# Router tables of the first two expert slots made on GpSimd instead of VectorE, with another deal of the last heads' products

## The chip, the cores and the metric

The kernel runs on one core of one Trainium2 chip. The metric is the device time of one launch in microseconds (us), the median of several runs. The core's engines are TensorE (PE in the profile, its weight loads PEld), VectorE (DVE), ScalarE (ACT), GpSimd (POOL) and SyncE (SP), which here only issues transfers. Each engine works through its own instructions in the order written, and waits for others by semaphores.

## What is computed

Attention with a threshold below each row's maximum, then a mixture of eight experts with one expert for each token, then a dense feed-forward network. The reference, shortened:

```python
# q, k, v: (4, 8, 576, 64); 2304 tokens of width 512
scores = q @ k.T / 8
scores = where(scores >= scores.max(-1) - tau, scores, -1e9)
x = softmax(scores) @ v                         # rows: tokens, columns: 8 heads x 64
logits = x @ w_gate + modality_bias[modality_id]
e_idx, gate_w = argmax(logits), softmax(logits)[e_idx]
for e in range(8):
    mask = e_idx == e
    out[mask] = gate_w[mask] * (relu(x[mask] @ w1[e]) @ w2[e])
h = out @ w_in
result = (h * sigmoid(1.702 * h)) @ w_out
```

## The kernel before, in words

**Attention** (`Attention.run`) works on 16 pairs of heads, four pairs to a batch of 576 tokens. A pair has nine units of 128 query rows; an iteration `it` of the loop handles two units, so there are 72 full iterations (`it` 0 to 71) and one that only drains; the last batch begins at `it` 54. In each iteration TensorE makes the score products of two units (`qk`, L244, eight matmuls, or twelve where a pair's last unit falls in it), transposes the weights of the iteration before (`trans`, L330 and following), and takes some products with the values from the queue `avq` (`av_items`, L374 and L380) and at most one row item from the queue `rowq`. VectorE makes each unit's maximum (L272) and, after ScalarE's exponential (L278), its mask (L302). Two units' scores are in flight, each in PSUM banks of its own, so score products wait for the mask of two units earlier.

A **row item** (`row_items`, L414) transposes 128 finished tokens of four heads back into rows on TensorE, together with their eight router logits; ScalarE copies them out (`xr`, L419), GpSimd multiplies them by the softmax's reciprocals (L422 for the rows `xrow`, L427 for the logits `lgt`), and SyncE writes the rows to DRAM (L433, two transfers). `xr` and `xrow` have two buffers each.

How much of each queue an iteration takes is a table by hand. For the last batch these are `AVL` (value products) and `ROWL` (row items), with one entry for each of `it` 54 to 72. What is left in the queues runs after the loop in `att.tail`, between the steps that prepare the first expert slot.

**The router** (`Router`) gives each token a place in slots of 512 tokens. The first two slots (phase "A") are filled from batches 0 to 2 while the last batch's attention runs. Its steps wait in a list `side`, from which `sides` takes a few at fixed points of each iteration; `None` in that list ends a turn. After batch 2's logits the list holds, in order: `NROW` empty turns, the expert choice (`gate_items`, VectorE), running sums (`pre`, GpSimd, L707), and `assign("A")`: `ranks` (three small matmuls, L742 to L744, copied by ScalarE into `rs` and `cnt`), then `pages`, `starts`, `limits`, `slots`, `inside`, `counted`, `places`, `digits`, which turn ranks into places, then `high`, `low` and `values`, which make one-hot rows `R` and `OL`, then `sum_up` (15 small matmuls, L893, on TensorE), and `lists`, which gives the token indices `igaA`. With these GpSimd gathers the first slot's rows from DRAM (L1080). From `pages` to `values` nearly all is VectorE's, mixed in between its maxima and masks.

After attention the **first expert slot** needs its gathered rows scaled (L1241, VectorE), transposed (L965, TensorE) and split into two parts (ScalarE and VectorE); then its first products (L993) start, and from there the expert slots and the dense network keep TensorE at work to the end.

The lines that the change touches are the tables (L32, L33), `row_items`, `sides`, and the closures of `assign`.

Of the kernel before, what the change touches and what calls it, by code (L numbers as in the profile page):

```python
# [21 lines left out]
NE = 8  # L22
# [9 lines left out]
AVL = (2, 2, 3, 5, 0, 2, 3, 2, 1, 2, 2, 3, 5, 0, 2, 3, 3, 2, 5)  # L32
ROWL = (1, 1, 1, 0, 1, 1, 1, 1, 1, 0, 0, 0, 0, 1, 1, 1, 1, 1, 1)  # L33
# [6 lines left out]
NBW = 6  # L40
# [9 lines left out]
class Attention:  # L50
# [347 lines left out]
    def row_items(self, b, hh):  # L398
# [153 lines left out]
class Router:  # L552
# [19 lines left out]
    def setup_items(self, tmp_pool):  # L572
# [25 lines left out]
        self.pages = T([128, NE], "pages")  # L598
        self.place = T([128, NB * PG // 128], "place")
# [36 lines left out]
        def order():  # L636
# [4 lines left out]
            nc.gpsimd.tensor_scalar_mul(self.pages, e, float(PG))  # L641

# [78 lines left out]
    def assign(self, ph, gate):  # L721
# [5 lines left out]
        t = {}  # L727
        T = lambda shape, name, dt=F32: wk.tile(shape, dt, name=name)
# [8 lines left out]
        R = T([128, n, 2, nh], "R", BF16)  # L737

# [9 lines left out]
        def pages():  # L748

            if not first:  # L750
                nc.vector.tensor_sub(cnt, cnt, self.lim)
# [4 lines left out]
            nc.vector.tensor_tensor(  # L756
                cmp, cnt.unsqueeze(2).broadcast_to([128, NE, top]), pg.unsqueeze(1).broadcast_to([128, NE, top]),
                op=ALU.is_ge if first else ALU.is_gt)
            yield
            nc.vector.tensor_reduce(out=f, in_=cmp, axis=AX.X, op=ALU.add)  # L760
            yield

        def starts():
            x = T([128, NE, NE], "fx")
            nc.vector.tensor_mul(x, self.before, f.unsqueeze(1).broadcast_to([128, NE, NE]))
            yield
            nc.vector.tensor_reduce(out=excl, in_=x, axis=AX.X, op=ALU.add)
            yield
            nc.vector.tensor_scalar(base, excl, float(PG), 1.0, op0=ALU.mult, op1=ALU.add)
            yield  # L770

        def limits():
            if first:
                nc.vector.tensor_scalar(self.lim, excl, -1.0, float(NA), op0=ALU.mult, op1=ALU.add)
                yield
                nc.vector.scalar_tensor_tensor(out=self.lim, in0=self.lim, scalar=0.0, in1=f, op0=ALU.max, op1=ALU.min)
                yield
                nc.vector.tensor_add(end, excl, self.lim)
                yield
                nc.vector.tensor_scalar_mul(self.lim, self.lim, float(PG))  # L780
                yield
            else:
                nc.vector.tensor_add(end, excl, f)
                yield
                nc.vector.tensor_sub(base, base, self.lim)
                yield
                self.range = self.c.tile([128, 2], I32, name="range")
                nc.vector.tensor_scalar(self.range[:, 1:2], end[:, NE - 1:NE], float(NB_STATIC), None, op0=ALU.max)
                yield

        def slots():
            cmp = T([128, ns, NE], "cmp")
            nc.vector.tensor_tensor(
                cmp, end.unsqueeze(1).broadcast_to([128, ns, NE]),
                self.iota[:, 0:ns].unsqueeze(2).broadcast_to([128, ns, NE]), op=ALU.is_le,
            )
# [3 lines left out]
            nc.vector.tensor_reduce(out=ef, in_=cmp, axis=AX.X, op=ALU.add)  # L800
            yield
            ei = self.c.tile([128, ns], I32, name="ei" + ph)
            nc.vector.tensor_scalar(ei, ef, float(NE - 1), None, op0=ALU.min)
# [38 lines left out]
        def inside():  # L842
            nc.vector.tensor_tensor(ok, rs, be(self.lim), op=ALU.is_lt if first else ALU.is_ge)
            yield
            nc.vector.tensor_mul(ok, ok, self.oh[:, 0:n])
            yield

        def counted():
            nc.vector.tensor_add(rs, rs, be(base))
            yield  # L850
            nc.vector.tensor_mul(ok, ok, rs)
            yield

        def places():
            pos = T([128, n], "pos")
            nc.vector.tensor_reduce(out=pos, in_=ok, axis=AX.X, op=ALU.add)
            yield
            pint = T([128, n], "pint", I32)
            nc.vector.tensor_scalar_add(pint, pos, -1.0)
# [3 lines left out]
        def digits():  # L863
            pint = t["pint"]
# [8 lines left out]
        def low(c0, c1):  # L873
            nc.vector.tensor_tensor(
# [4 lines left out]
        def high():  # L879
            nc.vector.tensor_tensor(  # L880
                R[:, :, 1, :], self.iota[:, 0:nh].unsqueeze(1).broadcast_to([128, n, nh]),
                plf[:, 0].unsqueeze(2).broadcast_to([128, n, nh]), op=ALU.is_equal,
            )
# [30 lines left out]
        def compact():  # L914
# [17 lines left out]

        rest = [] if first else [None]
# [649 lines left out]
```

## Time and profile before

| | |
|---|---|
| median of 3 runs | 935.27 us (934.87 to 935.39) |
| profiled execution | 936.12 us, its span 934.4 us, mean granted clock 0.995 |
| PE busy | 904.0 us, 97% of the span |
| DVE, ACT, POOL busy | 512.2 (55%), 446.8 (48%), 223.1 us (24%) |
| chain that ended last | PE 81%, issue 7%, DVE 4%, DMA 3%, ACT 2%, POOL 2% |
| PE idle from 260 to 300 us | 4.6 us of 40 |
| PE idle from 310 to 320 us | 4.5 us of 10 |

Times within the span count from its first instruction; 1.7 us of the profiled execution lie outside it. Busy shares are averages over stages that differ: the attention loop ends at about 309 us, the expert slots follow from about 319 us. A wait is put down to the instruction that released it. Durations on POOL are rough.

### The profile page before, as it was taken

The page shows a single profiled execution, that of the slowest core. Times are in us where ns is not written, and L with a number is a line of the kernel's source. Part 1 is how long each engine was busy: PE and PEld are TensorE (multiplying, and loading weights), DVE is VectorE, ACT ScalarE, POOL GpSimd, SP SyncE. Part 2 cuts the span into 40 slices and gives each one's busy share as a digit, 9 for nine tenths or more (in the row PEclk, how much of TensorE's full clock was granted, in tenths as well). Part 3 has the DMA queues.
Part 4 walks back from the last instruction along what each step waited for, and adds up shares of the span by engine and source line. Part 5 has one row for each costly group of instructions (what it writes and reads, how often), then busy time and mean ns, then how long its engine had stood idle before and what let it go on. Part 6 is the DMA issues. An engine that isn't in the chain of part 4 may idle for free.

```text
span 934.4 us, 13874 instructions
## 1 busy us (share of the span) xinstructions
PE 904.0 (97%) x5031; PEld 740.6 (79%) x5031; DVE 512.2 (55%) x1129; ACT 446.8 (48%) x788; POOL 223.1 (24%) x299
## 2 busy tenths in 40 slices
PE   8999999999998799999999999999999999999994
PEld 7777777777776588778888988888888888888894
DVE  6788788888789485477777568821111111211110
ACT  6677777777666443446455545532223222222221
POOL 4837556566602501010530000010001000100100
PEclk9999999999999999999999999999999999999998
DMA  7755774664411644466666244410001000100100
GB/s 211 174 145 148 204 199 115 156 164 119 109 43 26 206 141 143 153 204 203 196 207 233 94 140 147 150 46 1 25 22 46 6 12 6 46 1 1 46 1 25
DMA packets 64522, 100.70 MB, mean 108 GB/s; under 512 B 10596, under 2 KB 35970, under 8 KB 64450
## 3 DMA queue, kind: packets, MB, share of 16 engines
q1 hardware_dynamic: 61138, 89.84, 33.5%
q0 software_dynamic: 3312, 9.94, 3.2%
q8 instruction: 41, 0.67, 0.3%
q14 instruction: 31, 0.25, 0.1%
HBM read 63.97 MB, written 17.11 MB: 87 GB/s over the span
## 4 chain that ended last, share of the span: by engine, by line
PE 81%; issue 7%; DVE 4%; DMA 3%; ACT 2%; POOL 2%; SPq 1%; POOLq 0%; ACTq 0%
PE tr L993 28%; PE sc L1018 19%; PE sc L1037 9%; PE sc L244 8%; PE av L374 6%; PE tr L330 5%; PE av L380 2%; PE tr L414 2%; DVE e L272 1%; ACT e L278 1%; DMA cv_raw<-in_moe_w_in_dram 1%; SPq L179 1%; PE tr L352 1%; DVE E L302 1%; DMA xg<-y_first 1%
## 5 line engine op out<-in xcount | busy, mean ns | idle before, releaser
L1230 DVE TENSOR_TENSOR hl<-sg,hh 128x512 fp32r<-128x512 f32 (+1 forms) x80 | 51.1, 638 | 260.3 <-ACT hh L1228 257.9
L1227 ACT ACTIVATE sg<-tr 128x512 f32<-128x512 f32 (+1 forms) x80 | 44.3, 554 | 225.4 <-PE tr L993 225.4
L278 ACT ACTIVATE e<-e,thr 128x576 f32<-128x576 f32 x144 | 109.7, 776 | 77.4 <-DVE e L272 74.8
L272 DVE TENSOR_SCALAR_CACHE_REDUCE e<-sc,taue 128x576 f32<-128x576 f32 x144 | 113.4, 815 | 38.4 <-PE sc L244 37.7
L1018 PE MATMUL sc<-wo_h,hh 128*128 128x512 f32 x288 | 112.2, 390 | 0.0
L1018 PE MATMUL sc<-wo_l,hh 128*128 128x512 f32 x288 | 112.2, 390 | 0.0
L1018 PE MATMUL sc<-wo_h,hl 128*128 128x512 f32 x288 | 112.0, 389 | 0.0
L244 PE MATMUL sc<-kA,qT 128*128 128x288 f32 x320 | 99.3, 331 | 5.8 <-DVE E L302 3.8
L302 DVE SCALAR_TENSOR_TENSOR E<-sc,thr,e 128x576 f32<-128x576 f32 x128 | 100.7, 813 | 4.7 <-ACT e L278 3.8
L244 PE MATMUL sc<-kB,qT 128*128 128x288 f32 x320 | 87.9, 295 | 1.7 <-DMA kB<-kB 1.2
L993 PE MATMUL tr<-xl,wi_h 128*128 128x512 f32 (+1 forms) x320 | 78.7, 368 | 0.0
L993 PE MATMUL tr<-xh,wi_l 128*128 128x512 f32 (+1 forms) x320 | 78.7, 368 | 0.0
L993 PE MATMUL tr<-xh,wi_h 128*128 128x512 f32 (+1 forms) x320 | 78.6, 368 | 0.0
L374 PE MATMUL av<-AT,V 128*64 128x288 f32 x512 | 76.9, 419 | 0.5 <-ACT xT L381 0.5
L244 PEld LDWEIGHTS sc<-kA,qT 128*128 128x128 f32 x320 | 60.1, 188 | 21.0 <-DVE E L302 14.1
L332 ACT COPY AT<-tr 128x512 f32<-128x512 f32 x128 | 68.3, 577 | 0.1
L330 PE MATMUL tr<-ident,E 128*128 128x128 f32 x512 | 67.6, 272 | 0.0
L993 PEld LDWEIGHTS tr<-xh,wi_h 128*128 128x128 f32 x320 | 57.6, 188 | 11.1
L993 PEld LDWEIGHTS tr<-xh,wi_l 128*128 128x128 f32 x320 | 56.9, 189 | 10.0
L993 PEld LDWEIGHTS tr<-xl,wi_h 128*128 128x128 f32 x320 | 56.9, 189 | 10.0
L1018 PEld LDWEIGHTS sc<-wo_h,hl 128*128 128x128 f32 x288 | 54.0, 188 | 11.4
L244 PEld LDWEIGHTS sc<-kB,qT 128*128 128x128 f32 x320 | 60.2, 188 | 3.0 <-issue 1.3
(220 smaller groups left out, 1567.2 us busy)
## 6 DMA issues: line engine op xcount, KB each, us to landing
ra<-in_moe_w_dram SPq DMA_DIRECT2D x20, 512.0 KB
rb<-in_moe_w_dram SPq DMA_DIRECT2D x20, 512.0 KB, 5.2
F<-in_kq_dram SPq DMA_DIRECT2D x15, 640.0 KB, 4.6
cv_raw<-in_moe_w_in_dram SPq DMA_DIRECT2D x16, 512.0 KB, 4.8
cv_raw<-in_moe_w_out_dram SPq DMA_DIRECT2D x16, 512.0 KB, 4.3
V<-in_vp_dram SPq DMA_DIRECT2D x16, 320.0 KB, 5.0
kA<-kA SPq DMA_DIRECT2D x15, 320.0 KB, 3.3
kB<-kB SPq DMA_DIRECT2D x15, 320.0 KB, 3.6
```

What stands on the lines that cost most here:

```text
L244: m = nc.tensor.matmul(self.banks[:, bank, 0:288], l, d[kk][:, c0 + k0:c0 + k0 + 288], start=(i == 0), stop=(i == len(ops) - 1),).ins
L272: self.read(u, nc.vector.tensor_scalar(e, d["sc", w], self.taue[:, 0:1], 3.0e38, op0=ALU.add, op1=ALU.min, accum_out=thr))
L278: self.nc.scalar.activation(d["e", w], d["e", w], ACTF.Exp, bias=d["thr", w][:, 0:1], scale=-1.0)
L302: self.read(u, nc.vector.scalar_tensor_tensor(out=E.rearrange("p (a c) -> p a c", a=2), in0=d["sc", w], scalar=d["thr", w][:, 0:1], in1=d[ ...
L330: nc.tensor.transpose(tp[:, kc * 128:(kc + 1) * 128], E[:, k0 + kc * 128:k0 + (kc + 1) * 128], self.ident)
L332: return lambda: nc.scalar.copy(AT[:, h, :, c * 128:(c + 1) * 128], tp.rearrange("p (k c) -> p k c", k=4))
L374: nc.tensor.matmul(d["av"][h * 64:(h + 1) * 64, 0:288], d["V"][:, h, kc, :], d["AT"][:, h, kc, cols], start=(kc == 0), stop=False, skip_gr ...
L993: nc.tensor.matmul(hps[:, 0:T], w[:, kd, :], blk[x][:, kd, 0:T], start=(i == 0), stop=(i == 11))
L1018: nc.tensor.matmul(y, h[:, cs], w, start=(f == 0 and i == 0), stop=(f == blk["nf"] - 1 and i == 2))
L1037: nc.tensor.matmul(blk["y"][d], w[:, ds], h[:, 0:T], start=(f == 0 and i == 0), stop=(f == last and i == 2))
L1227: nc.scalar.activation(sg, hps, ACTF.Gelu_apprx_sigmoid)
L1230: return [upper, lambda: nc.vector.tensor_sub(hl, sg, hh.bitcast(F32))]
```

## The change

The steps from `pages` to `values` of phase "A" move from VectorE to GpSimd. GpSimd compares by a subtraction and a comparison with zero (`compare`), and sums along a row by halving (`fold`); `limits` takes seven instructions in place of four; `digits` counts the multiples of 128 below a place in place of an integer shift; and each of the 15 columns of `OL` is an instruction of its own with a scalar for each partition. `double` lets a point of `sides` take two of these steps. `NROW` empty turns become one for batch 2. A row item's logits are now made ahead of its rows. `False` in the list ends every point but an iteration's last, so that `sum_up` comes at an iteration's end. `AVL` and `ROWL` have new entries.

```diff
-AVL = (2, 2, 3, 5, 0, 2, 3, 2, 1, 2, 2, 3, 5, 0, 2, 3, 3, 2, 5)
-ROWL = (1, 1, 1, 0, 1, 1, 1, 1, 1, 0, 0, 0, 0, 1, 1, 1, 1, 1, 1)
+AVL = (2, 2, 3, 2, 3, 2, 3, 2, 1, 2, 2, 3, 3, 2, 2, 3, 3, 2, 5)
+ROWL = (0, 1, 0, 1, 1, 1, 1, 1, 1, 0, 0, 0, 0, 1, 0, 1, 0, 1, 0)
...
             nc.gpsimd.tensor_mul(
+                lgt[0:w, kc, hs, :].rearrange("p (a c) e -> p a c e", a=2),
+                xr[0:w, :, 128:144].rearrange("p a (c e) -> p a c e", c=2),
+                rr.unsqueeze(3).broadcast_to([w, 2, 2, NE]),
+            )
+            nc.gpsimd.tensor_mul(
                 xrow[0:w].rearrange("p (a c d) -> p a c d", a=2, c=2),
                 xr[0:w, :, 0:128].rearrange("p a (c d) -> p a c d", c=2),
                 rr.unsqueeze(3).broadcast_to([w, 2, 2, 64]),
-            )
-            nc.gpsimd.tensor_mul(
-                lgt[0:w, kc, hs, :].rearrange("p (a c) e -> p a c e", a=2),
-                xr[0:w, :, 128:144].rearrange("p a (c e) -> p a c e", c=2),
-                rr.unsqueeze(3).broadcast_to([w, 2, 2, NE]),
             )
             for u in range(2 if kc < 4 else 1):
                 nc.sync.dma_start(xd[b, 2 * kc + u][:, hh * 256:(hh + 1) * 256], xrow[u * 64:(u + 1) * 64, :])
...
-                self.side.extend([None] * NROW + items + self.router.after_batch(b, gate))
+                self.side.extend([None] * (1 if b == B - 2 else NROW) + items + self.router.after_batch(b, gate))
...
+            if f is False:
+                if not turn:
+                    break
+                side.pop(0)
+                continue
...
+            nc.gpsimd.tensor_scalar_mul(self.hundreds, e, 128.0)
...
+        def compare(out, x, y, op):
+
+            if not first:
+                return nc.vector.tensor_tensor(out, x, y, op=op)
+            nc.gpsimd.tensor_sub(out, x, y)
+            nc.gpsimd.tensor_scalar(out, out, 0.0, None, op0=op)
+
+        def fold(out, x):
+
+            if not first:
+                return nc.vector.tensor_reduce(out=out, in_=x, axis=AX.X, op=ALU.add)
+            m = x.shape[-1]
+            while m > 2:
+                k = m // 2
+                nc.gpsimd.tensor_add(x[:, :, 0:k], x[:, :, 0:k], x[:, :, m - k:m])
+                m -= k
+            nc.gpsimd.tensor_add(out, x[:, :, 0], x[:, :, 1])
...
-                nc.vector.tensor_scalar(self.lim, excl, -1.0, float(NA), op0=ALU.mult, op1=ALU.add)
+                E.tensor_scalar(self.lim, excl, -1.0, float(NA), op0=ALU.mult, op1=ALU.add)
                 yield
-                nc.vector.scalar_tensor_tensor(out=self.lim, in0=self.lim, scalar=0.0, in1=f, op0=ALU.max, op1=ALU.min)
+                more = T([128, NE], "more")
+                E.tensor_scalar(self.lim, self.lim, 0.0, None, op0=ALU.max)
                 yield
-                nc.vector.tensor_add(end, excl, self.lim)
+                E.tensor_sub(more, self.lim, f)
                 yield
-                nc.vector.tensor_scalar_mul(self.lim, self.lim, float(PG))
+                E.tensor_scalar(more, more, 0.0, None, op0=ALU.max)
+                yield
+                E.tensor_sub(self.lim, self.lim, more)
+                yield
+                E.tensor_add(end, excl, self.lim)
+                yield
+                E.tensor_scalar_mul(self.lim, self.lim, float(PG))
                 yield
...
+            if first:
+                pos, g = t["pos"], T([128, n, nh], "ge")
+                hundreds = self.hundreds.unsqueeze(1).broadcast_to([128, n, nh])
+                E.tensor_sub(g, pos.unsqueeze(2).broadcast_to([128, n, nh]), hundreds)
+                E.tensor_scalar(g, g, 0.0, None, op0=ALU.is_ge)
+                yield
+                fold(plf[:, 0], g)
+                E.tensor_scalar_add(plf[:, 0], plf[:, 0], -1.0)
+                yield
+                E.tensor_scalar_mul(plf[:, 1], plf[:, 0], 128.0)
+                E.tensor_sub(plf[:, 1], pos, plf[:, 1])
+                yield
+                return
...
         def low(c0, c1):
+            if first:
+                for c in range(c0, c1):
+                    nc.gpsimd.tensor_scalar(OL[:, c], self.iota, plf[:, 1, c:c + 1], None, op0=ALU.is_equal)
+                return
             nc.vector.tensor_tensor(
                 OL[:, c0:c1], self.iota.unsqueeze(1).broadcast_to([128, c1 - c0, 128]),
                 plf[:, 1, c0:c1].unsqueeze(2).broadcast_to([128, c1 - c0, 128]), op=ALU.is_equal,
             )
 
         def high():
-            nc.vector.tensor_tensor(
+            compare(
                 R[:, :, 1, :], self.iota[:, 0:nh].unsqueeze(1).broadcast_to([128, n, nh]),
-                plf[:, 0].unsqueeze(2).broadcast_to([128, n, nh]), op=ALU.is_equal,
-            )
+                plf[:, 0].unsqueeze(2).broadcast_to([128, n, nh]), ALU.is_equal)
 
         def values(i):
-            eng = nc.gpsimd if first and not i else nc.vector
-            eng.tensor_mul(R[:, :, i, :], R[:, :, 1, :], self.idp[:, i, 0:n].unsqueeze(2).broadcast_to([128, n, nh]))
+            E.tensor_mul(R[:, :, i, :], R[:, :, 1, :], self.idp[:, i, 0:n].unsqueeze(2).broadcast_to([128, n, nh]))
...
+        def double(g):
+
+            def go():
+                it, end = g(), object()
+                while next(it, end) is not end and next(it, end) is not end:
+                    yield
+
+            return go if first else g
...
-            None, ranks, pages, starts, limits, slots, inside, counted, places, digits, *rest, high,
+            None, ranks, *map(double, (pages, starts, limits, slots, inside, counted, places, digits)), *rest, high,
             lambda: (low(0, 5), values(0)), *rest, lambda: (low(5, 10), values(1)), *rest, lambda: low(10, n), gate,
-            *[None] * (1 if first else NBW), lambda: sum_up(0, n), lists,
+            *([None, False] if first else [None] * NBW), lambda: sum_up(0, n), lists,
```

Where the instructions stand now. On **TensorE in iteration 66**, the three matmuls of `ranks` follow the transposes, one iteration earlier than before (in iteration 67 they stood between the same kinds of rows); `oh` are the choices, `pre` their running sums, `tri` and `ones` constants, `tr` a PSUM bank. Now:

```order
L244 MATMUL sc<-kB,qT_137 128x288
L330 MATMUL tr<-ident,E 128x128 x8
L768 LDWEIGHTS tri
L768 MATMUL tr<-oh,tri 128x120
L769 LDWEIGHTS ones
L769 MATMUL tr<-pre,ones 128x120
L770 LDWEIGHTS ones
L770 MATMUL tr<-pre,ones 128x8
L374 MATMUL av<-AT,V 64x288 x6
```

Iteration 66 also has six of the value products' instructions in place of eight and their closing one (L380), which stand in iteration 67 now.

On **TensorE**, the 15 pairs of `sum_up` stood in **iteration 71**, behind that iteration's transposes (first pair shown):

```order
L244 MATMUL sc<-kA,qT_135 128x288
L244 MATMUL sc<-kB,qT_135 128x288
L330 MATMUL tr<-ident,E 128x128 x8
L893 LDWEIGHTS OL
L893 MATMUL tr<-R,OL 128x16
```

They now close **iteration 69**, ahead of iteration 70's score products:

```order
L330 MATMUL tr<-ident,E 128x128 x8
L374 MATMUL av<-AT,V 64x288 x4
L380 MATMUL av<-ATt,V 128x288
L414 MATMUL tr<-G,xT 128x144 x2
L945 LDWEIGHTS OL
L945 MATMUL tr<-R,OL 128x16
```

`sum_up` moved up by nearly two iterations; between `ranks` and `sum_up` lie iterations 67 to 69 and the end of 66.

On **POOL** there now stand 58 instructions between batch 2's running sums and the first row item of the last batch, where one stood among the row items before (L887, the second factor of `R`). Their last part:

```order
L911 TENSOR_TENSOR plf<-pos,plf 128x15
L751 TENSOR_TENSOR R<-iota,plf 128x15x8
L752 TENSOR_SCALAR R<-R 128x15x8
L926 TENSOR_SCALAR OL<-iota,plf 128x128 x5
L939 TENSOR_TENSOR R<-R,idp 128x15x8
L926 TENSOR_SCALAR OL<-iota,plf 128x128 x5
L939 TENSOR_TENSOR R<-R,idp 128x15x8
L926 TENSOR_SCALAR OL<-iota,plf 128x128 x5
L405 MEMSET lgt 64x64
L422 TENSOR_TENSOR lgt<-xr,r 128x32
L427 TENSOR_TENSOR xrow<-xr,r 128x256
L706 COPY g_3447<-g 128x80
```

The 58 are 32 of at most 64 elements for each partition, 11 of 120, and 15 of 128 (`OL`); nearly every one reads what the one before it wrote. Row items of the last batch stand behind them on POOL; in the loop three of its first five are left (`it` 67, 69 and 71), and two more follow in the tail, where there are now seven.

## Rows read from the trace of the kernel before

**Rows 1.** Windows: iterations 64 to 70 one by one, 71 with tail, first slot.

```profile
core 0: us, PE busy (x) PEld busy (x) DVE busy (x) ACT busy (x) POOL busy (x), PEclk, DMA share, GB/s
263.15:267.76 4.61, 3.43 (x26) 2.50 (x24) 4.12 (x13) 3.22 (x7) 0.00 (x0) 1.00 0.06 14
267.76:272.16 4.40, 4.11 (x29) 3.02 (x29) 4.37 (x16) 2.86 (x6) 1.01 (x6) 1.00 0.02 4
272.16:276.85 4.69, 4.69 (x36) 3.38 (x35) 3.45 (x11) 3.31 (x7) 0.14 (x1) 1.00 0.00 0
276.85:281.45 4.60, 3.72 (x30) 3.32 (x28) 2.71 (x9) 2.60 (x7) 0.00 (x0) 1.00 0.00 0
281.45:286.67 5.22, 4.53 (x33) 3.42 (x33) 5.12 (x21) 3.30 (x7) 0.81 (x2) 1.00 0.11 27
286.67:290.89 4.22, 4.22 (x33) 3.31 (x32) 4.06 (x17) 2.98 (x6) 0.81 (x2) 1.00 0.14 35
290.89:296.94 6.05, 4.54 (x38) 3.46 (x36) 5.98 (x18) 3.37 (x8) 1.67 (x3) 1.00 0.09 22
296.94:309.60 12.66, 12.17 (x97) 8.08 (x95) 6.66 (x21) 5.61 (x12) 6.22 (x9) 1.00 0.44 115
309.60:319.45 9.85, 5.32 (x38) 4.08 (x36) 3.80 (x6) 5.02 (x11) 3.71 (x7) 1.00 0.71 229
```

**Rows 2.** Timeline, TensorE: start, duration, line, operation, count, [idle before, its releaser].

```profile
242.72 0.40 PE L244 MATMUL sc<-kA,qT 128*128 128x288 f32 x1 [0.75 <-DVE ET L302]
...
273.42 1.04 PE L330 MATMUL tr<-ident,E 128*128 128x128 f32 x8
...
278.66 1.04 PE L330 MATMUL tr<-ident,E 128*128 128x128 f32 x8
...
280.29 0.76 PE L414 MATMUL tr<-G,xT 128*128 128x144 f32 x4 [0.48 <-ACT cnt L746]
...
296.44 0.76 PE L414 MATMUL tr<-G,xT 128*128 128x144 f32 x4 [1.51 <-ACT AT L332]
...
312.56 0.33 PE L965 MATMUL tr<-ident,xg 128*128 128x128 f32 x1 [2.47 <-DVE xg L1241]
...
319.45 1.20 PE L993 MATMUL tr<-xh,ah 128*128 128x512 f32 x4 [1.91 <-ACT xr L419]
```

**Rows 3.** Timeline, VectorE: first and last of 26 moved instructions, and one between.

```profile
280.27 0.18 DVE L756 TENSOR_TENSOR cmpp<-cnt,pages 128x24 f32<-128x24 f32 x1 [0.38 <-ACT cnt L746]
...
294.04 0.27 DVE L887 TENSOR_TENSOR R<-R,idp 128x120 bf16<-128x120 bf16 x1
...
294.97 0.81 DVE L874 TENSOR_TENSOR OL<-iota,plf 128x640 bf16<-128x640 f32 x1
```

**Rows 4.** Timeline, POOL: instructions of the kinds and sizes that the change adds.

```profile
56.40 0.62 POOL L633 TENSOR_SCALAR tri<-iota,pf 128x128 bf16<-128x128 f32 x1
...
77.19 0.53 POOL L651 TENSOR_TENSOR bias<-bias,tmpb 128x160 f32<-128x160 f32 x1
...
270.78 1.31 POOL L707 TENSOR_TENSOR pre<-pre,oh 128x8 bf16<-128x8 bf16 x5 [8.37 <-DVE r L311]
...
293.05 0.38 POOL L887 TENSOR_TENSOR R<-R,idp 128x120 bf16<-128x120 bf16 x1
```

**Rows 5.** Windows behind TensorE's last matmul; columns as in rows 1.

```profile
922.00:923.00 1.00, 0.46 (x3) 0.04 (x1) 0.51 (x1) 0.40 (x1) 0.32 (x1) 1.00 0.00 0
...
925.00:926.00 1.00, 0.00 (x0) 0.00 (x0) 0.00 (x0) 0.00 (x0) 0.00 (x0) 0.87 0.56 213
926.00:927.00 1.00, 0.00 (x0) 0.00 (x0) 0.00 (x0) 0.00 (x0) 0.00 (x0) 0.50 0.27 86
```

**Rows 6.** Timeline, POOL: two row items of the tail, the second slot's first gather.

```profile
313.97 0.61 POOL L422 TENSOR_TENSOR xrow<-xr,r 128x256 f32<-128x256 f32 x1 [6.18 <-ACT xr L419]
...
317.32 1.45 POOL L422 TENSOR_TENSOR xrow<-xr,r 128x256 f32<-128x256 f32 x1 [1.77 <-DMA x_dram<-xrow]
...
322.49 1.04 POOL L1080 DMA_INDIRECT xg<-x_dram,igaA  x1 [0.15 <-PE tr L993]
```

More of the change, by code (lines that the diff above doesn't have):

```diff
@@ L598, in setup_items @@
         self.pages = T([128, NE], "pages")
+        self.hundreds = self.wk["A"].tile([128, NA * PG // 128], F32, name="hundreds")
         self.place = T([128, NB * PG // 128], "place")
@@ L727, in assign @@
         t = {}
+        E = nc.gpsimd if first else nc.vector
         T = lambda shape, name, dt=F32: wk.tile(shape, dt, name=name)
@@ L750, in pages @@
             if not first:
-                nc.vector.tensor_sub(cnt, cnt, self.lim)
+                E.tensor_sub(cnt, cnt, self.lim)
                 yield
@@ L755, in pages @@
             pg = self.pages[:, 1:top + 1] if first else self.pages[:, 0:top]
-            nc.vector.tensor_tensor(
+            compare(
                 cmp, cnt.unsqueeze(2).broadcast_to([128, NE, top]), pg.unsqueeze(1).broadcast_to([128, NE, top]),
-                op=ALU.is_ge if first else ALU.is_gt)
+                ALU.is_ge if first else ALU.is_gt)
             yield
-            nc.vector.tensor_reduce(out=f, in_=cmp, axis=AX.X, op=ALU.add)
+            fold(f, cmp)
             yield
@@ L764, in starts @@
             x = T([128, NE, NE], "fx")
-            nc.vector.tensor_mul(x, self.before, f.unsqueeze(1).broadcast_to([128, NE, NE]))
+            E.tensor_mul(x, self.before, f.unsqueeze(1).broadcast_to([128, NE, NE]))
             yield
-            nc.vector.tensor_reduce(out=excl, in_=x, axis=AX.X, op=ALU.add)
+            fold(excl, x)
             yield
-            nc.vector.tensor_scalar(base, excl, float(PG), 1.0, op0=ALU.mult, op1=ALU.add)
+            E.tensor_scalar(base, excl, float(PG), 1.0, op0=ALU.mult, op1=ALU.add)
             yield
@@ L792, in slots @@
             cmp = T([128, ns, NE], "cmp")
-            nc.vector.tensor_tensor(
+            compare(
                 cmp, end.unsqueeze(1).broadcast_to([128, ns, NE]),
-                self.iota[:, 0:ns].unsqueeze(2).broadcast_to([128, ns, NE]), op=ALU.is_le,
-            )
+                self.iota[:, 0:ns].unsqueeze(2).broadcast_to([128, ns, NE]), ALU.is_le)
             yield
@@ L799, in slots @@
             ef = sh
-            nc.vector.tensor_reduce(out=ef, in_=cmp, axis=AX.X, op=ALU.add)
+            fold(ef, cmp)
             yield
             ei = self.c.tile([128, ns], I32, name="ei" + ph)
-            nc.vector.tensor_scalar(ei, ef, float(NE - 1), None, op0=ALU.min)
+            E.tensor_scalar(ei, ef, float(NE - 1), None, op0=ALU.min)
             yield
@@ L842, in inside @@
         def inside():
-            nc.vector.tensor_tensor(ok, rs, be(self.lim), op=ALU.is_lt if first else ALU.is_ge)
+            compare(ok, rs, be(self.lim), ALU.is_lt if first else ALU.is_ge)
             yield
-            nc.vector.tensor_mul(ok, ok, self.oh[:, 0:n])
+            E.tensor_mul(ok, ok, self.oh[:, 0:n])
             yield
         def counted():
-            nc.vector.tensor_add(rs, rs, be(base))
+            E.tensor_add(rs, rs, be(base))
             yield
-            nc.vector.tensor_mul(ok, ok, rs)
+            E.tensor_mul(ok, ok, rs)
             yield
@@ L855, in places @@
             pos = T([128, n], "pos")
-            nc.vector.tensor_reduce(out=pos, in_=ok, axis=AX.X, op=ALU.add)
+            fold(pos, ok)
             yield
+            if first:
+                E.tensor_scalar_add(pos, pos, -1.0)
+                yield
+                t["pos"] = pos
+                return
             pint = T([128, n], "pint", I32)
-            nc.vector.tensor_scalar_add(pint, pos, -1.0)
+            E.tensor_scalar_add(pint, pos, -1.0)
             yield
@@ L873, in low @@
         def low(c0, c1):
+            if first:
+                for c in range(c0, c1):
+                    nc.gpsimd.tensor_scalar(OL[:, c], self.iota, plf[:, 1, c:c + 1], None, op0=ALU.is_equal)
+                return
             nc.vector.tensor_tensor(
@@ L879, in high @@
         def high():
-            nc.vector.tensor_tensor(
+            compare(
                 R[:, :, 1, :], self.iota[:, 0:nh].unsqueeze(1).broadcast_to([128, n, nh]),
-                plf[:, 0].unsqueeze(2).broadcast_to([128, n, nh]), op=ALU.is_equal,
-            )
+                plf[:, 0].unsqueeze(2).broadcast_to([128, n, nh]), ALU.is_equal)
         def values(i):
-            eng = nc.gpsimd if first and not i else nc.vector
-            eng.tensor_mul(R[:, :, i, :], R[:, :, 1, :], self.idp[:, i, 0:n].unsqueeze(2).broadcast_to([128, n, nh]))
+            E.tensor_mul(R[:, :, i, :], R[:, :, 1, :], self.idp[:, i, 0:n].unsqueeze(2).broadcast_to([128, n, nh]))
         def sum_up(c0, c1):
```

7 lines of the change are left out of this document (4 added, 3 removed).

## Prediction, made before the run

> **What bounds the kernel now.** I first read the busy times in 40 slices: TensorE is at nine tenths or more in nearly all, and less only between 260 and 320 us, so a gain or loss must lie there. Then the windows by iteration of the last batch [rows 1]: the second number is TensorE's busy time, the fourth VectorE's. In iterations 64, 67, 68 and 70 VectorE is busy or in someone's way and TensorE idles 1.18, 0.88, 0.69 and 1.51 us (length less busy); in 66 and 69 TensorE is never idle and is itself the bound. The timeline then names the waits [rows 2]: masks, copies behind delayed masks, and in the first slot 2.47 us for the gathered and scaled rows and 1.91 us for a copy in the chain of row items. From 319.45, where the first expert products start, TensorE works nearly without a gap, so I count everything to that instant and let the rest of the kernel shift by as much.
>
> **Up to iteration 66.** The value products taken out of iteration 57 and given to 58 fill the 0.75 us that TensorE waited there [rows 2]. The expert choice of batch 2 comes one iteration earlier. Its nine VectorE instructions, the cause of the 1.18 and 0.29 us idle in iterations 64 and 65 [rows 1], now fall beside iterations with more TensorE work, but VectorE is nearly full in either place; I count a gain of 0.25 there. Gain 1.0, bounds 0 and 2.2: iteration 66 starts at 272.16 - 1.0 = 271.2. Making `lgt` ahead of `xrow` exchanges two instructions on POOL that both have to be done; it lets the choice start without the wait for a buffer, and I cost it at nothing.
>
> **TensorE from 66 to `sum_up`.** Before, iterations 66 to 69 took 272.16 to 290.89, 18.73 us, of which 0.88 + 0.69 = 1.57 idle [rows 1]. With the 26 instructions off VectorE (7.8 us in all, first and last in [rows 3]) these waits go. `ranks` and the value products only move within the stretch. The row item of iteration 68 moves to the tail: 296.44 to the next score product at 296.94, 0.5 us [rows 1, 2]. So TensorE would need 18.73 - 1.57 - 0.5 = 16.6 us and reach the 15 matmuls of `sum_up`, now at the end of 69, at 271.2 + 16.6 = **287.8**.
>
> **GpSimd's chain.** It can start when `cnt` is copied. Before, that ended TensorE's wait at 280.29, 3.44 us into iteration 67 [rows 2]; iteration 66 has four score products fewer, and its transposes start 1.26 us after its start instead of 1.81 [rows 1, 2], so 2.9 us: 271.2 + 2.9 = 274.1. The chain has 58 instructions, nearly each waiting for the last:
> - 32 small ones at 0.262, the step of the five dependent sums (1.31 us, [rows 4]): 8.4 us.
> - 11 of 120 elements: 0.38 for `R` [rows 4] and 0.07, near what dependence adds to the sums, 0.45 each: 5.0 us.
> - 15 columns of `OL`. The `tri` table is the same instruction in all: 128 numbers against one scalar for each partition, to bf16, 0.62 us [rows 4]: 9.3 us.
>
> Together **22.7 us**. From below: 0.20 and 0.38 without the step, 6.4 + 4.2 + 9.3 = 19.9. From above: the 0.53 of a plain product of 160 [rows 4] plus 0.07 for the 11, 8.4 + 6.6 + 9.3 = 24.3. I take the middle one, since the sums show the step in a chain of this very kind. POOL has at most 0.81 us of work in each of iterations 66 to 69 [rows 1], so nothing else is in its way. `OL` is ready at 274.1 + 22.7 = **296.8**.
>
> So TensorE, which takes its instructions in order, would stand at `sum_up` from 287.8 to 296.8: a **new wait of 9.0 us** (6.2 to 10.6 by the bounds). Behind it on TensorE is all of iteration 70, and behind that VectorE and ScalarE. On POOL the row items of 67 and 69, the gates' copy and then the four gathers queue behind the chain; SP's writes of them queue behind POOL, and so do the first slot's weights. These have some 20 us until they are used, so I cost that queue at nothing.
>
> **From `sum_up` to the first expert product.** Before, from the start of iteration 70 to 319.45: 28.56 us, with `sum_up` inside. Off go the 1.51 idle in 70 and its row item, 0.5. The gather's wait of 2.47 goes: `igaA` is made in iteration 70, not 71, ahead of some 12 us of TensorE work. The 1.91 us I let go too, since the first two row items of the tail no longer stand behind the gathers. On come two more row items in the tail, 1.0. That leaves 28.56 - 1.51 - 0.5 - 2.47 - 1.91 + 1.0 = 23.2 us: the first expert product at 296.8 + 23.2 = 320.0, **0.55 us later** than before.
>
> **The clock.** After the last matmul (its end 0.46 us into that window) the granted clock fell from 1.00 to 0.50, from 2.4 to 1.2 GHz; the 0.87 between puts the fall at 925.74, 3.3 us after it [rows 5]. No shorter wait in [rows 1] shows a fall. A wait of 9 us is long enough for it; a rise under load is in no row. The price lies between nothing and iteration 70 wholly at half rate, its 4.5 us of work again [rows 1]; between ends so alike I take the middle, **2.3 us**. The Trainium skill, TensorE: Matmul & The Clock Gate, section "What's actually happening", says that the throttled clock is the default and that only activity releases it; by that rule the end at nothing would fall away and the sum would be no lower than 2.3.
>
> **The sum.** 0.55 + 2.3 = 2.85 us on the profiled execution's 936.12, 939.0. The median of the runs is 0.85 below that execution, so **938.1**.
>
> **Rivals.**
> - *GpSimd is quick enough* (faster). `values` ran on both engines: 0.27 us on VectorE, 0.38 on POOL [rows 3, 4], 1.4 times. If the whole table scaled like that, 7.8 x 1.4 = 10.9 us would fit into the 13.7 us from 274.1 to 287.8, `sum_up` would not wait, and the first expert product would come at 287.8 + 23.2 = 311.0: 8.4 us earlier, 926.8. It decides below a chain of 13.7 us without a wait; with one, and no loss of clock, below 22.1. For it: that one pair of rows. Against: 58 instructions stand for 26, and `tri`'s 0.62 alone makes 9.3. Chance 0.17. The Trainium skill, GPSIMD Engine Reference, section 3.1, gives about 1.96 for such a product, an estimate of 15.2 us for the table; by that rule the wait is 1.5 us and the time 928.3. The rows of `values` agree with a ratio under two, the rows of `OL` don't: 0.81 for five columns on VectorE against five times 0.62.
> - *The wait comes, but costs nothing in the end* (no change). The chain is near its lower end or the clock is back at once: -2.25 at 19.9 us and no loss, +0.55 at 22.7, so 933.0 to 935.8. For it: 5 us of later waits go. Chance 0.2.
> - *The tail becomes the bound too* (slower). Seven row items instead of five wait for `xrow`'s two buffers and their writes; two of them took 3.35 us on POOL from 313.97 to 317.32, and the second slot's gathers stand behind them [rows 6]. If the two more delay the first product, or later the second slot's scaling, by 3.35: 941.4. Against: they start without waiting for a gather. Chance 0.13.
>
> **How the numbers follow.** Forecast 0.50, rivals 0.17, 0.20 and 0.13. A measurement of this kernel tells about 0.2%, 1.9 us, from no change. Of the forecast's half I put 0.45 beyond that, so slower 0.45 + 0.13 = 0.58, near nothing otherwise; of the second rival 0.03 is beyond it, faster 0.17 + 0.03 = 0.20; the rest, 0.22, is the same. The bounds of the chain and the clock give 933.0 to 936.12 + 2.15 + 4.5 - 0.85 = 941.9; I set 931.5 to 942, for a gain up to 66 at its upper bound. The quick chain stays outside.
>
> **What would show it.** In the changed kernel's trace: `OL`'s columns near 0.62 us each and POOL busy over 20 us without a break from about 274 us; an idle time of 6 to 11 us before the first matmul of `sum_up`, released by POOL; a granted clock under 1.00 right behind it; no idle over 0.5 us on TensorE in iterations 67 and 68; no wait for gathered rows before the first slot. The prediction is wrong if POOL is done when TensorE arrives, or if iterations 67 to 69 take as long as the chain for another reason.

## The result and the profile after

The changed kernel takes 943.06 us (median of 5 runs, 940.63 to 944.98), the kernel before 935.27 (5 runs, 934.87 to 937.16): ratio 1.0081, interval 1.006 to 1.0103. That is slower, as forecast, but 7.8 us where 2.8 were forecast, and above the range. The profiled execution took 944.39 us, its span 942.6 against 934.4, 8.2 more.

On the page, TensorE's busy time grows by 4.9 us and GpSimd's by 19.4, VectorE's falls by 6.0, and the row of the granted clock has a dip in the 13th and 14th slice (283 to 330 us):

```profile
PE 908.9 (96%) x5031; PEld 744.1 (79%) x5031; DVE 506.2 (54%) x1103; ACT 446.8 (47%) x788; POOL 242.5 (26%) x357
...
PEclk9999999999997899999999999999999999999998
```

The timeline of TensorE shows the two places (columns as in [rows 2]):

```profile
271.56 0.51 PE L244 MATMUL sc<-kA,qT 128*128 128x288 f32 x1
...
287.35 0.65 PE L414 MATMUL tr<-G,xT 128*128 128x144 f32 x4
295.47 0.42 PE L945 MATMUL tr<-R,OL 128*128 128x16 bf16 x10 [7.47 <-POOL R L939]
...
298.37 0.20 PE L945 MATMUL tr<-R,OL 128*128 128x16 bf16 x1 [0.39 <-POOL OL L926]
298.42 0.59 PE L244 MATMUL sc<-kA,qT 128*128 128x288 f32 x1
...
304.44 0.40 PE L244 MATMUL sc<-kA,qT 128*128 128x288 f32 x1
...
323.80 1.11 PE L1026 MATMUL tr<-ident,xg 128*128 128x128 f32 x4 [2.54 <-ACT xr L419]
...
325.99 2.08 PE L1054 MATMUL tr<-xh,ah 128*128 128x512 f32 x4
```

Iteration 66 starts at 271.56; TensorE is done with iteration 69 at 288.0 and starts iteration 70 at 298.42. In between it is idle 7.47 us, and 1.71 more column by column, as `OL` comes. The second place is the tail: 2.54 us in front of the first slot's last transposes. The kernel before had 1.91 just behind these, and 2.47 in front of an earlier transpose [rows 2]. The first expert product starts at 325.99, 6.54 us later than before, and the second layer's first at 336.31 against 327.74, 8.57 later. The last matmul starts 7.86 later (929.93 against 922.07), so little changes behind that: a wait of 1.40 us at 395.93 of the kernel before is one of 0.69 here, at 403.75.

Windows of the changed kernel (columns as in [rows 1]) show the clock at both places:

```profile
290.00:292.00 2.00, 0.00 (x0) 0.00 (x0) 0.00 (x0) 0.00 (x0) 2.00 (x5) 1.00 0.00 0
292.00:293.00 1.00, 0.00 (x0) 0.00 (x0) 0.00 (x0) 0.00 (x0) 1.00 (x3) 0.87 0.00 0
300.00:302.00 2.00, 2.00 (x11) 1.98 (x11) 1.91 (x8) 1.14 (x2) 0.38 (x1) 0.50 0.30 69
303.00:304.00 1.00, 1.00 (x10) 0.59 (x10) 0.37 (x2) 0.65 (x2) 0.00 (x0) 1.00 0.37 92
318.00:320.00 2.00, 1.93 (x15) 1.71 (x16) 0.88 (x2) 1.70 (x5) 1.73 (x5) 1.00 1.04 368
323.00:324.00 1.00, 0.20 (x1) 0.21 (x2) 0.00 (x0) 0.40 (x1) 1.00 (x3) 0.73 0.00 0
325.00:327.00 2.00, 2.00 (x6) 1.43 (x7) 0.69 (x1) 0.84 (x2) 0.81 (x2) 0.50 0.40 98
331.00:332.00 1.00, 1.00 (x6) 0.78 (x6) 0.34 (x1) 0.97 (x2) 0.69 (x2) 1.00 0.30 70
```

It falls within both waits (a mean of 0.87 puts the first fall at 292.7, one of 0.73 the second at 323.5) and is at 0.50 for most of iteration 70, until 303.0, and under the first expert products, until 330.3.

On GpSimd the chain runs without a gap from 274.50 to 298.3, and the tail's row items wait for row buffers:

```profile
274.50 0.23 POOL L751 TENSOR_TENSOR cmpp<-cnt,pages 128x24 f32<-128x24 f32 x1 [6.71 <-ACT cnt L772]
...
295.39 2.92 POOL L926 TENSOR_SCALAR OL<-iota,plf 128x128 bf16<-128x128 f32 x5
...
304.15 1.31 POOL L1141 DMA_INDIRECT xg<-x_dram,igaA  x1 [3.78 <-DVE E L302]
...
309.88 0.62 POOL L427 TENSOR_TENSOR xrow<-xr,r 128x256 f32<-128x256 f32 x1
...
322.70 0.61 POOL L427 TENSOR_TENSOR xrow<-xr,r 128x256 f32<-128x256 f32 x1 [2.81 <-DMA x_dram<-xrow]
```

And SP, which issues transfers in order, sends the first slot's weights behind iteration 71's row item, and that row item stands behind all four gathers on GpSimd: at 312.97, not 306.94 as before. The tail's row writes start at 318.75, where the windows show 368 GB/s. Of the writes whose landing the trace has, one of the first took 3.6 us, one of the next 2.8, later ones about 2; in the kernel before they took 2.1 in this stretch:

```profile
301.99 9.62 SPq L433 DMA_DIRECT2D x_dram<-xrow  x4
312.97 0.42 SPq L1310 DMA_DIRECT2D ra<-in_moe_w_dram  x1
...
318.75 11.75 SPq L433 DMA_DIRECT2D x_dram<-xrow  x12
```

### The profile page after: what moved, and what is told of

Read it like the earlier page. It is cut to its first block, busy times and chain, and to the rows that moved or that the text cites. A ratio compares the mean times of both kernels' runs of the same rounds, so it can differ in the third digit from the quotient of the medians.

```text
span 942.6 us, 13901 instructions
## 1 busy us (share of the span) xinstructions
PE 908.9 (96%) x5031; PEld 744.1 (79%) x5031; DVE 506.2 (54%) x1103; ACT 446.8 (47%) x788; POOL 242.5 (26%) x357
## 4 chain that ended last, share of the span: by engine, by line
PE 80%; issue 7%; POOL 4%; DVE 3%; DMA 3%; ACT 1%; SPq 1%; POOLq 0%; ACTq 0%
PE tr L1054 28%; PE sc L1079 18%; PE sc L1098 8%; PE sc L244 8%; PE av L374 6%; PE tr L330 5%; PE tr L414 2%; PE av L380 2%; POOL OL L926 1%; DVE e L272 1%; DMA cv_raw<-in_moe_w_in_dram 1%; SPq L179 1%; DMA qT<-kB 1%; PE tr L352 1%; DVE E L302 1%
```

## The experiments

Theory A: GpSimd's chain makes the wait at `sum_up`, two more row items with two row buffers make the tail's, and each takes the clock down. The rivals stand with each run. Every ratio is to the kernel before on the same chip (its median 936.1 to 936.5 there).

**1. The deal without the engine** (the kernel before, with these edits and the new order of `lgt` and `xrow`; all others but 6 and 10 start from the changed kernel)

```diff
-AVL = (2, 2, 3, 5, 0, 2, 3, 2, 1, 2, 2, 3, 5, 0, 2, 3, 3, 2, 5)
-ROWL = (1, 1, 1, 0, 1, 1, 1, 1, 1, 0, 0, 0, 0, 1, 1, 1, 1, 1, 1)
+AVL = (2, 2, 3, 2, 3, 2, 3, 2, 1, 2, 2, 3, 3, 2, 2, 3, 3, 2, 5)
+ROWL = (0, 1, 0, 1, 1, 1, 1, 1, 1, 0, 0, 0, 0, 1, 0, 1, 0, 1, 0)
...
-                self.side.extend([None] * NROW + items + self.router.after_batch(b, gate))
+                self.side.extend([None] * (1 if b == B - 2 else NROW) + items + self.router.after_batch(b, gate))
```

> The changed deal alone (new AVL and ROWL, one empty turn, logits ahead of rows), with the whole table on VectorE as before. Theory A (GpSimd's chain makes the wait at sum_up, the two more row items of the tail make a second, smaller one): sum_up finds its tables within 1 us, the granted clock stays at 1.00 up to 316 us, so all of the first loss is gone; what the deal costs alone is the tail's wait. 933 to 936 us if the tail then waits under 2 us, up to 939 if it waits 2.5 us and the clock falls there too. Rival B (the deal, not the engine, is what costs): 941 us or more, with an idle time of over 5 us on TensorE before 310 us.

934.33 us, ratio 0.9982 (0.9969 to 0.9994). No fall of the clock in its profile. TensorE's waits at `sum_up` and in the tail, and the start of the tail's row items (TensorE) and of the weights (SP):

```profile
292.33 0.54 PE L893 MATMUL tr<-R,OL 128*128 128x16 bf16 x15 [1.17 <-ACT AT L332]
...
306.65 1.29 PE L414 MATMUL tr<-G,xT 128*128 128x144 f32 x8
...
313.97 0.66 PE L965 MATMUL tr<-ident,xg 128*128 128x128 f32 x4 [2.75 <-ACT xr L419]
...
303.20 0.42 SPq L1249 DMA_DIRECT2D ra<-in_moe_w_dram  x1
```

The deal by itself wins slightly. What costs is the table on GpSimd: run 8, with `sum_up` at the same place as here, has 1.0075, about 9 us more. But the tail's wait is here too, without GpSimd's chain, and GpSimd waits 3.02 us for a row buffer: this wait comes with the deal.

**2. `OL` back on VectorE**

```diff
-            if first:
-                for c in range(c0, c1):
-                    nc.gpsimd.tensor_scalar(OL[:, c], self.iota, plf[:, 1, c:c + 1], None, op0=ALU.is_equal)
-                return
             nc.vector.tensor_tensor(
...
-            lambda: (low(0, 5), values(0)), *rest, lambda: (low(5, 10), values(1)), *rest, lambda: low(10, n), gate,
-            *([None, False] if first else [None] * NBW), lambda: sum_up(0, n), lists,
+            *([lambda: values(0), lambda: values(1), gate, None, False,
+               lambda: (low(0, 5), low(5, 10), low(10, n), sum_up(0, n))] if first else [
...
```

> The 15 columns of OL go back to VectorE as three instructions, behind the masks of iteration 69; all else of the table stays on GpSimd. Theory A: R and both products of values are done about 290 us, OL (3 x 0.81 us from 287.9 on) about 290.5, so TensorE's wait from 288.0 shrinks from 10.4 to about 2.5 us, the clock does not fall there, and the time falls by 7.9 + 2.3 to about 933 us (the tail unchanged). Rival B (the wait only moves: to the gathers, or to the tail): the wait at sum_up shrinks as said, but the time falls by less than 5 us, to 938 or more.

935.56 us, ratio 0.9998 (0.9986 to 1.0009), 7.8 less than the changed kernel by the two ratios; some 10 were expected.

```profile
289.48 0.52 PE L941 MATMUL tr<-R,OL 128*128 128x16 bf16 x15 [3.08 <-POOL R L935]
...
291.00:292.00 1.00, 1.00 (x7) 0.99 (x6) 1.00 (x4) 0.40 (x1) 0.49 (x1) 0.50 0.24 60
...
315.26 1.12 PE L1024 MATMUL tr<-ident,xg 128*128 128x128 f32 x4 [3.06 <-ACT xr L419]
```

The wait shrinks as said, but the clock falls after 3.08 us too, and the tail's wait grows, with a second fall (0.50 from 314.5 to 321.4).

**3. More row buffers**

```diff
-        self.rp = Q("a_rows", 2)
+        self.rp = Q("a_rows", 3)
+        self.wp = Q("a_xrow", 4)
...
-            xrow = self.rp.tile([128, DM // 2], F32, name="xrow")
+            xrow = self.wp.tile([128, DM // 2], F32, name="xrow")
```

> The changed kernel with four buffers for xrow and three for xr in place of two each. Theory A (in the tail GpSimd waits 2.81 us for a row buffer's write, ScalarE for GpSimd, TensorE 2.54 us for ScalarE, and then the clock is at half until 330.1): sum_up's wait stays at 10.4 us, the tail's 2.54 us fall under 1 us, the clock stays at 1.00 there, and the time falls by 2.5 + 3 to about 937.6 us. Rival B (the writes or the first slot's weights are late by themselves, so another wait takes its place): 941 us or more.

938.92 us, ratio 1.0031 (1.0019 to 1.0043): 4.7 less than the changed kernel. The clock stays at 1.00 in the tail.

```profile
321.26 0.66 PE L1027 MATMUL tr<-ident,xg 128*128 128x128 f32 x4 [0.58 <-ACT xr L420]
```

So the number of row buffers makes the second loss, the wait and the fall behind it together, and its size is about 5 us.

**4. TensorE kept at work, in part**

```diff
+            if it == 69:
+                warm = self.ps_av.tile([128, 512], F32, name="av")
+                for _ in range(64):
+                    nc.tensor.transpose(warm[:, 0:128], self.ident, self.ident)
```

> 64 transposes of the identity (0.13 us each, 8.3 us, result not used) stand ahead of sum_up, so that TensorE works through most of its wait. Theory A (the idle time takes the clock down, and the price of that is the work done at half rate up to 303 us, 2.3 us): sum_up ends at the same time, 298.4 us, the clock is 1.00 behind it, and the time falls by about 2.3 us to 940.8; with the tail starting 2.3 us earlier and unchanged. Rival B (the clock costs nothing, since later waits take it up): 942.5 us or more, the tail's waits longer by what was won.

941.45 us, ratio 1.005 (1.0035 to 1.0065). The size is as expected, the way is not: `sum_up` still waited for its last columns, and the clock fell behind it, later and for less long:

```profile
300.00:301.00 1.00, 1.00 (x9) 1.00 (x9) 0.25 (x1) 0.00 (x0) 0.92 (x4) 1.00 0.00 0
301.00:302.00 1.00, 1.00 (x8) 1.00 (x8) 1.00 (x4) 0.33 (x1) 0.92 (x3) 0.70 0.00 0
303.00:304.00 1.00, 1.00 (x6) 0.53 (x6) 1.00 (x4) 1.00 (x3) 0.00 (x0) 0.50 0.27 36
```

The tail's wait stayed, at 2.58 us, with a fall behind it. This run doesn't settle the price of the clock; the ninth was made for that.

**5. `OL` on VectorE, more row buffers** (the edits of 2 and 3)

> OL on VectorE (as in the second experiment) and four buffers for xrow, three for xr (as in the third). Theory A (two losses of separate cause, which add): the wait at sum_up stays near 3.1 us with its clock fall, the tail's 3.06 us fall to about 0.6 and the second fall (half rate from 314.2 to 321.8) goes; 2.5 + 3 less than the second experiment's 935.6, about 930 us, so 0.994 of the kernel before. Rival B (with an earlier tail the row writes meet the weights' loads and the wait stays): 934 or more.

931.98 us, ratio 0.9952 (0.9937 to 0.9968). The waits are 2.99 and 0.58 us, with the first clock fall and without the second: the two losses add.

**6. The deal, more row buffers** (the edits of 1 and 3)

> Table on VectorE with the new deal (as in the first experiment) and the larger row buffers. Theory A: the tail's wait of 2.75 us falls to about 0.6, no clock fall was there to win back, so 2.2 less than the first experiment's 934.3: 932.1, or 0.996 of the kernel before. Rival B (that wait is hidden by another, the weights' split or the gathered rows): 934 or more.

929.36 us, ratio 0.9923 (0.9908 to 0.9938): faster than both kernels. No fall in its profile; 0.58 us in the tail. By the ratios it gained 5.5 us over the first, 3.3 more than expected. The first's runs spread from 932.2 to 937.4, with mean clocks from 0.996 down to 0.991, so in some of them the clock may have fallen in the tail; only a quick one was profiled.

**7. The old row items**

```diff
-ROWL = (0, 1, 0, 1, 1, 1, 1, 1, 1, 0, 0, 0, 0, 1, 0, 1, 0, 1, 0)
+ROWL = (1, 1, 1, 0, 1, 1, 1, 1, 1, 0, 0, 0, 0, 1, 1, 1, 1, 1, 1)
```

> The changed kernel with the old ROWL: row items again in iterations 68 and 70, five in the tail. Theory A (two more items in the tail make its wait long enough for the second clock fall): sum_up's wait stays over 9 us, the tail's last wait is 1.9 us or less, the clock stays at 1.00 there, and the time is 3 to 5 us under the changed kernel's, 938 to 940. Rival B (row copies now stand behind GpSimd's chain on ScalarE, which has two buffers of xr, and hold up the exponentials of iteration 70): ScalarE waits for GpSimd until 298 us, nothing is won, 942 or more.

941.37 us (939.09 to 943.67), ratio 1.0057 (1.0038 to 1.0075), less won than theory A said. The profile, of the quickest run, has a wait of 1.71 us in the tail and no second fall:

```profile
322.46 1.20 PE L1054 MATMUL tr<-xh,ah 128*128 128x512 f32 x4 [1.71 <-ACT xr L419]
```

Three of the slower ones have lower mean clocks (0.986 to 0.988, where it has 0.990) and no profile, so whether the second fall came back in them is not shown.

**8. `sum_up` half an iteration later**

```diff
-            *([None, False] if first else [None] * NBW), lambda: sum_up(0, n), lists,
+            *([None, None] if first else [None] * NBW), lambda: sum_up(0, n), lists,
```

> The changed kernel with sum_up in the middle of iteration 71, where the kernel before has it, in place of the end of iteration 69. Theory A (the chain is 24 us long whatever stands beside it, and TensorE is sent to its end 10 us early): TensorE does iteration 70 and half of 71 first, reaches sum_up at about 295 and waits 3 to 4 us instead of 10.4, so 6 to 7 less, and up to 2.3 more if the clock stays: 934.5 to 937. Rival B (the chain's end sets the first slot: its rows come so late that the wait moves to the gathers): the wait at sum_up shrinks as said, but TensorE waits over 3 us for the gathered rows, and the time is 940 or more.

943.58 us, ratio 1.0075 (1.0059 to 1.0092): nothing won. The edit put `sum_up` into the middle of iteration 70, not 71 as the expectation has it, so TensorE came 2.1 us later (18.6 after iteration 66's start, not 16.4). The wait shrank by that, and came back in the tail:

```profile
294.47 0.42 PE L945 MATMUL tr<-R,OL 128*128 128x16 bf16 x10 [5.37 <-POOL R L939]
...
322.77 1.12 PE L1026 MATMUL tr<-ident,xg 128*128 128x128 f32 x4 [5.15 <-ACT xr L419]
```

The first expert product came 54.45 us after iteration 66's start, in the changed kernel 54.43. The wait did move, as rival B said, but to the row buffers, not to the gathered rows: GpSimd waited 5.42 us for one.

```profile
321.67 0.61 POOL L427 TENSOR_TENSOR xrow<-xr,r 128x256 f32<-128x256 f32 x1 [5.42 <-DMA x_dram<-xrow]
```

Counted from iteration 66, the tail's row items started 2.6 us earlier here (314.26 on GpSimd, 317.91 in the changed kernel), the weights only 0.2 (311.72 and 312.97), so more of the writes lay among them. GpSimd's wait for a row buffer goes with the distance from the first weights' issue to the tail's first row item on TensorE: 1.77 us at 5.8 in the kernel before, 2.8 to 3.3 at 3.2 to 3.7 in the changed kernel and runs 1, 2 and 4, 5.42 at 1.3 here.

**9. TensorE kept at work to the end** (the edit of 4 with 90 in place of 64, and that of 3)

> Four row buffers (third experiment) and 90 transposes ahead of sum_up in place of 64: at 0.114 us each (7.3 us for 64 in the fourth experiment) 10.3 us, as long as the whole wait from 288.0 to 298.4. Theory A (the first clock fall comes from the idle time and costs the half-rate work behind it): the granted clock stays at 1.00 all the way, iteration 70 takes about 4 us in place of the changed kernel's 6.0, and the time is about 2 us under the third experiment's 938.9, about 937. Rival B (the fall is not from idle time, or what it costs is taken up by a later wait): a clock of 0.50 in iteration 70 all the same, or 938.5 or more.

940.49 us (936.2 to 943.22), ratio 1.0036 (1.0021 to 1.0051), no better than the third.

```profile
286.77 10.04 PE L506 MATMUL av<-ident 128*128 128x128 f32 x90
...
297.21 0.38 PE L245 MATMUL sc<-kA,qT 128*128 128x288 f32 x1
...
301.83 0.40 PE L245 MATMUL sc<-kA,qT 128*128 128x288 f32 x1
...
300.00:302.00 2.00, 2.00 (x15) 1.00 (x15) 1.48 (x5) 1.76 (x4) 0.00 (x0) 1.00 0.34 56
...
334.59 0.23 PE L774 MATMUL tr<-pre,ones 128*128 128x160 bf16 x1 [2.84 <-POOL pre L719]
...
336.00:337.00 1.00, 1.00 (x3) 0.75 (x3) 0.00 (x0) 0.13 (x1) 0.00 (x0) 0.50 1.04 398
```

The clock stays at 1.00 from the transposes to 335.5: iteration 70 takes 4.62 us with 0.50 idle, in the changed kernel 6.02. So idle time took the clock down, and the first fall costs 6.02 - 4.12 = 1.9 us at its place. The second layer also starts 1.5 us earlier after iteration 66 than in the third (58.49 against 60.00). Then 2.84 us are lost in a wait that the third has not: the last batch's running sums are late on GpSimd, behind a row item that waited 4.43 us for its buffer, and behind that wait the clock falls after all (0.50 from 335.5 to 339.0). Theory A holds for the clock at its place, rival B for the median time. The profiled run (942.34) is one of the slower ones; three of the twelve lie at 936.2 to 937.7, about where theory A put them, and whether the late wait stands in these is not shown.

**10. The kernel before, more row buffers** (the edit of 3)

> The kernel before with four buffers for xrow and three for xr, nothing else. Theory A (five row items in the tail wait for their writes too, 1.91 us on TensorE, but without a clock fall): that wait falls to about 0.6, 1.3 us are won at most, 0.9985 to 1.0. Rival B (the buffers are worth as much here as with the new deal, 5 us, so the gain of the sixth experiment is theirs alone): 0.995 or less.

936.02 us, ratio 0.9999 (0.9985 to 1.0013): nothing, so the gain of the sixth is not the buffers' alone. Here TensorE's wait for a row copy shrinks to 0.60, but the one for gathered rows is 4.04, with the clock at 0.50 behind it (313.7 to 317.1), and the first expert product starts at 319.44, as before:

```profile
312.75 0.33 PE L966 MATMUL tr<-ident,xg 128*128 128x128 f32 x1 [4.04 <-DVE xg L1242]
...
314.00:315.00 1.00, 1.00 (x6) 0.88 (x5) 0.43 (x1) 0.47 (x2) 0.85 (x3) 0.50 0.25 90
```

The buffers are worth 5 us only with the new deal; with the old one the gather's wait takes up what they give.

**11. `OL` on VectorE, `sum_up` in the middle of 70** (the edits of 3 and 2, with `sum_up` in a turn of its own)

> OL on VectorE at the end of iteration 69, the rest of the table on GpSimd, sum_up in the middle of iteration 70, larger row buffers. Theory A: TensorE reaches sum_up 2.4 us later than in the fifth experiment, waits about 0.7 us instead of 3.0, and the clock stays; 2.3 + 1.5 less than its 932.0: about 928, 0.991 to 0.992 of the kernel before. Rival B (VectorE, held by plf until 288 us, is late with iteration 70's maxima and masks, and the wait moves to iteration 71's score products): 931 or more.

931.67 us, ratio 0.9945 (0.9932 to 0.9957), as the fifth. Rival B's cause, at another place: VectorE waits 0.36 us for `plf` and makes `OL` in 2.75, ahead of iteration 70's maxima, so ScalarE's exponentials wait 3.04 us and its copies come late. The wait stands at `sum_up`, not in iteration 71, and the clock falls there (0.50 from 292.5 to 295.9):

```profile
292.58 0.55 PE L942 MATMUL tr<-R,OL 128*128 128x16 bf16 x15 [3.52 <-ACT AT L333]
```

**12. Two of four weight loads later**

```diff
-    for g in range(2):
-        for i in range(2):
-            blocks[0]["load"](g, i)
+    for i in range(2):
+        blocks[0]["load"](0, i)
...
             blocks[0]["split"](0, 0)
+            for j in range(2):
+                blocks[0]["load"](1, j)
```

> The changed kernel with two of the first slot's four weight loads (ra and rb of the second group) issued behind the tail's second transposes instead of ahead of its row items; row buffers as they were. Theory A (the tail's 2.81 us for a row buffer is a row write that lies among 2 MB of weights): the row writes of 318 to 320 us land in about 2 us, GpSimd waits 1.8 us or less for the buffer, TensorE's wait shrinks from 2.54 to about 1.5, the second clock fall goes, and the time is 3 to 4 us under the changed kernel's: 939 to 941. Rival B (a write takes that long by itself): the waits stay at 2.5 and 2.8, 942.5 or more.

945.23 us, ratio 1.0092 (1.0078 to 1.0106), no faster. In the tail it went part of theory A's way: GpSimd's wait is 1.58 us, TensorE's 1.96, and the second fall half as long (322.4 to 325.8). But a later row write then met the moved loads:

```profile
321.81 0.66 PE L1026 MATMUL tr<-ident,xg 128*128 128x128 f32 x4 [1.96 <-ACT xr L419]
...
323.00:324.00 1.00, 1.00 (x5) 0.61 (x4) 0.69 (x1) 0.09 (x1) 0.00 (x0) 0.50 0.46 115
...
330.53 0.89 POOL L427 TENSOR_TENSOR xrow<-xr,r 64x256 f32<-64x256 f32 x1 [4.37 <-DMA x_dram<-xrow]
...
338.48 0.23 PE L769 MATMUL tr<-pre,ones 128*128 128x160 bf16 x1 [2.52 <-POOL pre L714]
```

The running sums made TensorE wait 2.52 us, with a third fall behind it (339.5 to 342.9). A row write among weights takes longer: where the trace has the landing, it is 2.1 us for the writes of 319 to 324 us, and 3.9 at 325 to 327, behind the moved loads of 323.93 and 324.54. Moving the weights moves the wait.

## Why the prediction was wrong

- **Up to `sum_up`: right.** Iteration 66 began 0.60 us earlier (1.0 forecast), TensorE was there at 288.0 (287.8), and idle in 67 and 68 is gone.
- **GpSimd's chain: right, at the upper part of its bounds.** 274.50 to 298.3 is 23.8 us (22.7 forecast, 19.9 to 24.3). The first 22 small instructions took 6.52 us, from 274.50 to 281.02, 0.296 each (0.262); the next five, of 120 elements, 2.53 us, 0.51 each (0.45); the 15 columns 8.77 us, 0.585 each (0.62). The rival of a quick GpSimd is out: 23.8 for VectorE's 7.8 is a ratio of 3.05. The Trainium skill's 1.96 (GPSIMD Engine Reference, section 3.1), by which the estimate was 15.2 us, was measured on one add of 2048 fp32 elements. It does not carry over to this table, which takes 58 small instructions for 26.
- **The new wait: right.** 9.18 us idle (9.0).
- **The first clock fall: right.** 1.9 us at its place (2.3 forecast); the ninth run shows idle time as its cause. With that agrees what the Trainium skill says (TensorE: Matmul & The Clock Gate, "What's actually happening"), that the throttled clock is the default and activity releases it. (That the sum would be "no lower than 2.3" by that rule does not follow: the rule only excludes a price of nothing.)
- **From `sum_up` to the first expert product: the step that failed.** "The 1.91 us I let go too, since the first two row items of the tail no longer stand behind the gathers": the wait didn't go, it was 2.54. The gathered rows no longer hold the tail back, and its seven row items write among the first slot's weights with two buffers. The gather's wait of 2.47 [rows 2] had given the weights time to land: before, the tail's first row item on TensorE came 5.8 us behind the first weights' issue (312.72 and 306.94), now 3.7 (316.68 and 312.97). More row buffers take this wait down to 0.58 (run 3). The late queue through GpSimd and SP, which the prediction cost "at nothing", is not what made it: in run 1, with the table on VectorE, the weights are issued at 303.20, the distance is 3.45 and the wait 2.75. The third rival had row buffers and writes as its mechanism, at 3.35 us and a chance of 0.13.
- **The clock, counted at one place: also failed.** The tail's 2.54 us took it down a second time, which is in no term of the prediction. "No shorter wait in [rows 1] shows a fall" was true, but no bound. Four transposes, a row item and three groups of products at half rate cost 3.0 us (0.97 from 323.80 to the first expert product, by the third run's 1.22 for the same, and 2.03 from there to the second layer, 10.32 against 8.29).

The sum to the second layer's first product: forecast 2.85; the chain's end 1.6 later (iteration 70 from 298.42, not 296.8); first fall 0.4 less; the tail's wait 2.5 more; the rest up to the first expert product 1.0 less (0.4 of it is `sum_up`, done but for its last column while TensorE waited; the other 0.6 is what is left over, not traced further); second fall 3.0 more: 8.55, measured 8.57. The 1.6, the 0.4 and the 1.0 nearly cancel, which is luck; the tail's wait and the second fall are what is left. TensorE has as many instructions as before (x5031) and 4.9 us more busy time, as much as the two falls together. With the third rival's 3.35 and the second fall's measured 3.0 the text would have come to 944.4. The range, up to 942, took the chain and the first fall at their upper ends, with neither of these added.

## What to carry to other kernels

Work that moves to an idle engine has to be timed as a chain, count by step, against the moment at which its reader arrives; and where a wait is removed, see which transfers it gave time to: here row writes ran into weights, and a gain upstream came back there as a longer wait (run 8). A wait of a few us on TensorE can cost the work behind it at half rate besides: 1.9 and 3.0 us here. Three runs that shortened one wait (8, 9 and 12) won nothing, since a later one, for a row buffer or for what stood behind it on GpSimd, took it. Adding row buffers under the new deal (3, 5 and 6) and bringing `OL` forward (2) kept most or all of their gain.

## What was not expected of the hardware

The length of a wait alone does not order the falls: 2.54 us idle in the changed kernel's tail ended with the clock at 0.50, 2.75 us in run 1 did not, 3.06 in run 2 did. In run 12 the clock fell 0.6 us behind a wait of only 1.96, with TensorE at work again. In run 4 too it fell while TensorE was busy, about 1.5 us behind the last of six waits of 0.19 to 0.40. What decides between 2 and 3 us stays open; no run was made for it.
